# Sink attention followed by mixture-of-experts attention on one core: two-bank PSUM buffers evacuated as wholes, values in pairs of rows, and a new order of steps

## The chip, the core and the metric

The kernel runs on one core of a Trainium2 chip. The metric is device time in microseconds (us) of one execution. The kernel before took 470.62, 473.53 and 476.29 us in three runs, a median of 473.53. Its engines are PE (TensorE: matmuls, with PEld as its weight loads), DVE (VectorE), ACT (ScalarE), POOL (GpSimd) and SP (SyncE, which issues all DMAs). Matmul results land in PSUM, which here is cut into buffers; DVE and ACT can read them, POOL cannot.

## What is computed

Two attention layers, one after the other, in fp32. The first has 4 batches of 8 heads, 768 positions and a head size of 64; each position sees the 4 first positions ("sinks") and the last 128. Its output, with the heads side by side, is the x of the second.

```
scores = q @ k.T / 8;  keep = (pos_k < 4) | (0 <= pos_q - pos_k < 128)
a = softmax(where(keep, scores, -1e9));  x = a @ v          # x: 4 x 768 x 512
logits = x @ w_gate                                          # 4 experts, the best 2 are kept
w = softmax over the kept logits
for e in experts:
    q, k, v = x @ wq[e], x @ wk[e], x @ wv[e]                # 512 -> 64
    ye = softmax(causal(q @ k.T / 8)) @ v @ wo[e]
    out += w[e] * ye
```

## The kernel before

**Precision.** A product that needs fp32 is made of three matmuls of a split number: each operand is a high part (rounded) and a low part (the rest), and high x high, high x low and low x high are added up in PSUM (the tuple `THREE`). So every copy of such an operand out of PSUM is two instructions: ACT writes the high part, DVE subtracts it for the low part.

**Units of work.** `first(b, hp)` is the first attention for one batch and one pair of heads: 4 x 4 units. It loads q, k and v, turns q and k (in the first batch by PE, later by DVE), and works through six rows of 128 queries. `values(b)` multiplies x with wv and the gate weights for all six rows, then ranks the experts on DVE. `second(b, ep)` is the second attention for one pair of experts: 4 x 2 units. It first projects x to q and k, then works through six causal rows. `store(b, i)` multiplies the result by wo, two rows of 128 at a time, and sends them out.

A row of either attention passes PE four times in effect: scores (L497), transposing the probabilities (L545), attention times values (L518), with softmax between the first two: mask and minimum on DVE (L642, L709, L744), exponential on ACT (L650, L714, L748), reciprocal on DVE, scaling by POOL (L657, L721, L763). After the transposes ACT or DVE copies the result to SBUF (L395, L397). In the first attention two rows beyond the second go together (`both_rows`).

**PSUM.** There are three buffers named `s` of 1024 fp32 columns, which are two banks each, and two named `acc` of one bank, for attention times values. Everything else that PE writes goes to an `s` buffer: scores of a row (one bank for each head), transposes, projections, values and stores. One of them is taken when its first step is placed, and is free when its last user is done.

- A projection (L836, in `second`) has one `s` buffer for q and one for k. Four row blocks (512 columns) fill the first bank with 12 matmuls, the last two blocks (256 columns) half of the second with 12 more. `pair.put` then copies: ACT L442 the high part, DVE L445 the low part, once for 512 columns and once for 256. Its destination is written with a pattern of four dimensions.
- Values (L867) put one row into each bank, 12 matmuls of 260 columns; after each row its 256 value columns are copied (L395 or L397) and its 4 gate columns (L875).
- Stores (L912) put one row into each bank, 12 matmuls of 512 columns, each copied to an `o` tile (L395 or L397) and sent.

In each of these, the copies of the first bank depend on the matmuls of that bank alone.

**The order.** The whole program is recorded as steps (`plan.step`) with a priority, a cost in ns for each engine that can do it, the steps it follows and the buffers it takes or uses. `Plan.emit` then runs through them once and puts them in an order for every engine, always the step that can begin first; on PE a step's key is its priority, plus `STAY` if it changes the kind of matmul, plus `HURRY` for every 100 ns that PE would wait. Each engine then runs its instructions strictly in that order. Priorities come from a table of some thirty numbers near L931 (`LEAD_*`, `WIDE_*`, `PREP_*`, `UNIT_*`, `STORE` and so on) and from two strings, `ORD` and `LAST`, which say how the units of `first` (a digit), the second attention of the batch before (`p`) and of the last batch (`c`) take turns. The costs in these steps are the planner's alone; they set nothing but the order.

The semaphores that hold the engines back are put in by the framework below, from the order and from the tiles that the instructions touch.

## Time and profile before

| | us |
|---|---|
| runs shown | 470.62, 473.53, 476.29 (median 473.53) |
| the profiled execution | 475.6 |
| its span, first to last instruction | 473.6 |
| busy in it: PE | 415.6 (88%) |
| busy: DVE, ACT, POOL | 312.0, 289.1, 264.4 |
| mean granted clock of PE | 0.948 |

How to read it: a span is cut into groups of instructions by source line (L836 is line 836 of the kernel before). "Idle before" is time in which the engine had nothing to run just before an instruction, put down to the instruction on another engine whose end released it. The granted clock is 1.0 at full speed; at 0.5 PE runs at half its rate. The chain of work is the path of instructions and waits that ended last, followed back from the end.

### The profile page before, as it was taken

How to read it: one execution, taken by the hardware profiler on the slowest of the kernel's cores; microseconds unless marked ns; L12 is line 12 of the kernel's file. 1: busy time of each engine (PE TensorE's matmuls, PEld its weight loads, DVE VectorE, ACT ScalarE, POOL GpSimd, SP SyncE). 2: the span in 40 equal slices, each digit the busy share in tenths (PEclk: the TensorE clock that was granted, in tenths of full speed). 3: DMA queues.
4: the chain of work that ended last, by engine and by line, in shares of the span. 5: the costliest groups of instructions: out<-in, count | busy, mean ns of one | idle time of the engine just before them, and what ended most of it. 6: DMA issues, size and time to landing. Idle time of an engine off the chain costs nothing.

```text
span 473.6 us, 12733 instructions
## 1 busy us (share of the span) xinstructions
PE 415.6 (88%) x4516; PEld 337.9 (71%) x4516; DVE 312.0 (66%) x1280; ACT 289.1 (61%) x922; POOL 264.4 (56%) x406
## 2 busy tenths in 40 slices
PE   6779989989879998999879998799879978999985
PEld 5668768877657777868657777678658766787773
DVE  4887975679929985459829985459835731546752
ACT  4897975468847976149947882428925822414840
POOL 8677986857785776037875764327821620007840
PEclk9767987989989999999999999999997998999999
DMA  8997662271054124232054100031000000003012
GB/s 177 225 151 135 125 133 36 35 134 37 1 90 78 35 36 69 60 125 52 3 83 85 35 3 1 1 134 36 3 0 1 1 1 0 3 24 113 1 46 89
DMA packets 124031, 28.41 MB, mean 60 GB/s; under 512 B 120576, under 2 KB 120576, under 8 KB 123968
## 3 DMA queue, kind: packets, MB, share of 16 engines
q1 hardware_dynamic: 123968, 27.61, 27.9%
q8 instruction: 35, 0.57, 0.5%
q14 instruction: 28, 0.23, 0.2%
HBM read 21.05 MB, written 6.29 MB: 58 GB/s over the span
## 4 chain that ended last, share of the span: by engine, by line
PE 62%; DVE 20%; ACT 11%; issue 5%; POOL 2%; DVEq 0%; ACTq 0%; POOLq 0%
PE s L836 15%; PE acc L518 13%; PE s L497 10%; PE s L912 8%; PE s L867 7%; PE s L545 7%; DVE p L642 3%; ACT pt L395 3%; DVE pt L585 2%; ACT p L650 2%; DVE p L744 2%; ACT p L748 2%; DVE pt L397 1%; DVE s L737 1%; DVE qs L445 1%
## 5 line engine op out<-in xcount | busy, mean ns | idle before, releaser
L497 PE MATMUL s<-ks,qs 64*128 64x260 f32 (+4 forms) x960 | 102.6, 336 | 11.6 <-ACT pt L395 3.2
L497 PEld LDWEIGHTS s<-ks,qs 64*128 64x128 f32 x960 | 74.7, 202 | 29.2 <-DVE st L709 5.9
L657 POOL TENSOR_TENSOR p<-p,st 128x128 f32<-128x128 f32 (+5 forms) x96 | 87.5, 933 | 2.7
L395 ACT ACTIVATE pt<-s 128x512 f32<-128x512 f32 (+1 forms) x132 | 67.9, 534 | 34.2 <-PE s L545 13.5
L537 POOL TENSOR_TENSOR st<-st,gate 128x2 f32<-128x2 f32 x48 | 9.2, 195 | 118.5 <-DVE gate L899 62.7
L650 ACT ACTIVATE p<-p,st 128x128 f32<-128x128 f32 (+5 forms) x96 | 63.5, 662 | 12.8 <-DVE st L642 12.0
L545 PE MATMUL s<-ident,p 64*128 64x64 f32 x1120 | 59.7, 234 | 3.5 <-POOL p L721 0.7
L545 PEld LDWEIGHTS s<-ident,p 64*128 64x128 f32 x1120 | 47.2, 144 | 15.0 <-issue 8.1
L642 DVE CUSTOM_DVE_ANT_0 p<-s,cmask 128x512 f32<-128x512 f32 (+3 forms) x96 | 50.2, 551 | 8.7 <-PE s L497 7.3
L748 ACT ACTIVATE p<-p,st 128x132 f32<-128x132 f32 x128 | 50.4, 399 | 0.4 <-DVE st L744 0.2
L518 PE MATMUL acc<-pt,v 128*64 128x128 f32 x672 | 48.9, 284 | 0.8 <-ACT pt L395 0.6
L836 PE MATMUL s<-x,wkh 128*128 128x256 f32 (+1 forms) x128 | 36.7, 373 | 13.1 <-ACT ks L442 6.8
L518 PE MATMUL acc<-pt,vn 128*64 128x128 f32 x448 | 45.8, 305 | 0.0
L836 PE MATMUL s<-x,wqh 128*128 128x256 f32 (+1 forms) x128 | 34.9, 358 | 12.0 <-ACT qs L442 6.4
L518 PEld LDWEIGHTS acc<-pt,v 128*64 128x64 f32 x672 | 36.2, 138 | 7.6 <-ACT pt L395 1.9
L867 PE MATMUL s<-wvh,x 128*128 128x260 f32 x192 | 38.3, 291 | 1.4 <-DVE v L397 0.5
L445 DVE TENSOR_TENSOR ks<-s,ks 128x384 fp32r<-128x384 f32 (+2 forms) x24 | 13.2, 553 | 38.7 <-PE s L836 29.4
L912 PE MATMUL s<-woh,y 128*128 128x512 f32 x96 | 33.7, 407 | 4.4 <-ACT o L395 2.1
L836 PEld LDWEIGHTS s<-x,wkh 128*128 128x128 f32 x128 | 23.6, 203 | 19.5 <-ACT ks L442 8.4
L836 PEld LDWEIGHTS s<-x,wqh 128*128 128x128 f32 x128 | 21.6, 190 | 18.2 <-ACT qs L442 7.8
L867 PEld LDWEIGHTS s<-wvh,x 128*128 128x128 f32 x192 | 30.7, 188 | 3.8 <-DVE gate L875 1.5
L763 POOL TENSOR_TENSOR p<-p,st 128x512 f32<-128x512 f32 x32 | 33.3, 1039 | 0.0
(116 smaller groups left out, 912.6 us busy)
## 6 DMA issues: line engine op xcount, KB each, us to landing
vn<-in_v_dram SPq DMA_DIRECT2D x32, 192.0 KB, 3.0
out_dram<-o SPq DMA_DIRECT2D x24, 256.0 KB, 2.0
qn<-in_q_dram SPq DMA_DIRECT2D x52, 96.0 KB, 2.3
kn<-in_k_dram SPq DMA_DIRECT2D x52, 96.0 KB, 2.3
qn<-in_q_dram SPq DMA_DIRECT2D x6, 192.0 KB, 4.1
kn<-in_k_dram SPq DMA_DIRECT2D x6, 192.0 KB, 4.4
o<-in_moe_wo_dram SPq DMA_DIRECT2D x2, 256.0 KB, 4.3
v<-in_moe_wv_dram SPq DMA_DIRECT2D x4, 128.0 KB, 2.8
```

What stands on the lines that cost most here:

```text
L395: nc.scalar.activation(dst(), src(), AF.Copy)
L497: nc.tensor.matmul(o, self.qs.t[hs, a, qs], self.ks.t[hs, b, ks], start=n == 0, stop=n == 2)
L518: nc.tensor.matmul(o[e * 64:e * 64 + 64], lhs, rhs, start=e not in self.begun, stop=last and i == self.hi - 1)
L545: nc.tensor.transpose(t.t[:, g, n, :], x[gs], ident[gs, gs])
L642: nc.vector.tensor_tensor_reduce(out=p.t[:, cs], in0=s2.t[:, e, :(c1 - c0) * 128], in1=mask[:, cs], scale=times, scalar=st.t[:, 3, es] if ...
L650: nc.scalar.activation(x, x, AF.Exp, bias=st.t[:, 0, es], scale=-1.0, accum_out=st.t[:, 1, es])
L657: nc.gpsimd.tensor_mul(x, x, st.t[:, 2, e:e + 1].to_broadcast([128, n * 128]))
L748: nc.scalar.activation(p.t[:, n, :], p.t[:, n, :], AF.Exp, bias=st.t[:, 0, n:n + 1], scale=-1.0, accum_out=st.t[:, 1, n:n + 1])
L763: nc.gpsimd.tensor_mul(p.t[:, :, :128], p.t[:, :, :128], f()[:, :, None].to_broadcast([128, 4, 128]))
L836: nc.tensor.matmul(t.t[:, at:at + n], w[a][:, c, es], X[b, c].t[:, x, cs], start=c == 0 and m == 0, stop=c == NCH - 1 and m == 2)
L867: nc.tensor.matmul(ps()[:, :VW], X[b, c].t[:, a, qs], W["wv"][w][:, c, :], start=c == 0 and n == 0, stop=c == NCH - 1 and n == 2)
L912: nc.tensor.matmul(t.t[:, r, :], Y[b, c].t[:, a, qs], W["wo"][w][:, c, :], start=c == 0 and n == 0, stop=c == EP - 1 and n == 2)
```

## The change

- In `second`, the projections of both parts of a buffer come first; the four copies follow, each waiting for the last matmul of **both** parts. The copies' source and destination are flat (`flat=True`), two dimensions in place of four.
- In `values`, nothing is copied after the first row of a buffer. After the second, one instruction copies 2 x 256 value columns and one copies 2 x 4 gate columns. The second row's matmuls follow the first's.
- In `store`, both rows' matmuls come first, then both copies.
- The planner's table of numbers is another one: costs of transposes (for instance 109 to 62 ns a block), of the switch between kinds of matmul, of ranking, the priorities, and the two strings of turns. The work of the instructions themselves does not change by it, only their order.

The core of the diff; of the table two lines stand for the rest:

```diff
-        def put(self, which, lo, hi, src, t, prio, after):
+        def put(self, which, lo, hi, src, t, prio, after, flat=False):
...
             def to(a):
+                if flat:
+                    return self.tile(which).t[:, a, lo * 128:hi * 128]
                 return self.part(which, a, lo, hi).rearrange("p j (g c) -> p j g c", c=64)
...
-            t = buf("s", 1024)
+            t, puts = buf("s", 1024), []
...
-                new, used = pair.fresh(which)
+                new, used = ([], [pair.tile(which)]) if lo else ([pair.tile(which)], [])
...
-                pair.put(which, lo, hi, lambda t=t, n=n, at=at: t.t[:, at:at + n].rearrange("p (j g c) -> p j g c", g=2, c=64), t, prep_prio, [last])
+                puts.append((lo, hi, lambda t=t, n=n, at=at: t.t[:, at:at + n], t, prep_prio, last))
+            for lo, hi, src, t, prep_prio, _ in puts:
+                pair.put(which, lo, hi, src, t, prep_prio, [x[-1] for x in puts], flat=True)
...
-                made, last = i % 2 == 0, None
+                made, before, last = i % 2 == 0, None if i % 2 == 0 else last, None
...
-                V2_READY[b].append(evacuate(prio, lambda i=i: v2.t[:, i, :], lambda ps=ps: ps()[:, :E * D], E * D, [last],
-                                            [t, v2]))
-                logits.append(plan.step(prio, {DVE: 190}, lambda i=i, ps=ps: nc.vector.tensor_copy(
-                    gate.t[:, 0, i, :], ps()[:, E * D:VW]), [last], [gate] if i == 0 else [], [t] + ([gate] if i else [])))
+                if made:
+                    continue
+                V2_READY[b] += [evacuate(prio, lambda i=i: v2.t[:, i - 1:i + 1, :], lambda t=t: t.t[:, :, :E * D], 2 * E * D, [before, last],
+                                         [t, v2])] * 2
+                logits.append(plan.step(prio, {DVE: 190}, lambda i=i, t=t: nc.vector.tensor_copy(
+                    gate.t[:, 0, i - 1:i + 1, :], t.t[:, :, E * D:VW]), [before, last], [gate] if i == 1 else [], [t] + ([gate] if i > 1 else [])))
...
-                                 [last] + [x for cc in range(EP) for x in over(Y_READY[b, cc], i + r, i + r + 1)] + W_READY["wo"],
+                                 [last, before] + [x for cc in range(EP) for x in over(Y_READY[b, cc], i + r, i + r + 1)] + W_READY["wo"],
                                  [t] if made else [], [Y[b, c]] + ([] if made else [t]), mode="FULL")
+            before = last
+            done.append((r, o, qs))
+        for r, o, qs in done:
             moved = evacuate(prio + 0.1 * r, lambda o=o: o.t, lambda r=r: t.t[:, r, :], Dm, [last], [t], [o])
...
-    WIDE_S, WIDE_E, WIDE_N = 16.27, -11.64, 15.51
+    WIDE_S, WIDE_E, WIDE_N = 14.65, 1.07, 15.16
...
-    LAST = "1 0 p0 2 3 p1 c0 c1"
+    LAST = "0 p0 1 2 3 p1 c0 c1"
```

What it does to the order is shown at three places. In these rows a name ends in its buffer's number (`s_120`, `s_121`, `s_122` are the three two-bank buffers); the semaphores in brackets are those that the row waits for, by the engine that raises them; lines of the changed kernel stand some three to seven further down (L836 is L839 there, L442 is L445, L497 is L500).

PE, the second bank (256 columns) of the q projection of the last unit, and the first matmul of the k projection behind it; before:

```order
L836 MATMUL s_122<-x_76,wqh 128x256 x2
L836 MATMUL s_122<-x_76,wql 128x256
L836 MATMUL s_122<-x_77,wqh 128x256 [waits Activation_49]
L836 MATMUL s_122<-x_77,wqh 128x256
L836 MATMUL s_122<-x_77,wql 128x256
L836 MATMUL s_122<-x_79,wqh 128x256 x2
L836 MATMUL s_122<-x_79,wql 128x256
L836 MATMUL s_122<-x_78,wqh 128x256 [waits DVE_49]
L836 MATMUL s_122<-x_78,wqh 128x256
L836 MATMUL s_122<-x_78,wql 128x256
L836 MATMUL s_120<-x_76,wkh 128x512 x2
```

and now:

```order
L839 MATMUL s_121<-x_76,wqh 128x256 x2
L839 MATMUL s_121<-x_76,wql 128x256
L839 MATMUL s_121<-x_77,wqh 128x256 x2
L839 MATMUL s_121<-x_77,wql 128x256
L839 MATMUL s_121<-x_79,wqh 128x256 x2
L839 MATMUL s_121<-x_79,wql 128x256
L839 MATMUL s_121<-x_78,wqh 128x256 x2
L839 MATMUL s_121<-x_78,wql 128x256
L839 MATMUL s_122<-x_76,wkh 128x512 [waits DVE_49]
```

The two waits inside the buffer are gone. One wait stands at the start of the next buffer, for its last user.

ACT, the copies of the same unit's q and k and what follows them; before:

```order
L442 ACTIVATE qs_72<-s_122 128x512 [waits PE_49]
L442 ACTIVATE qs_72<-s_122 128x256 [waits DVE_49,PE_49]
L442 ACTIVATE ks_75<-s_120 128x512 [waits PE_49]
L442 ACTIVATE ks_75<-s_120 128x256 [waits DVE_49,PE_49]
L650 ACTIVATE p_88,st_119<-p_88,st_119 128x384 [waits DVE_49]
```

and now:

```order
L445 ACTIVATE qs_72<-s_121 128x512 [waits PE_49]
L445 ACTIVATE qs_72<-s_121 128x256
L445 ACTIVATE ks_75<-s_122 128x512 [waits PE_49]
L445 ACTIVATE ks_75<-s_122 128x256
L396 ACTIVATE pt_99<-s_120 128x512 [waits DVE_49,PE_49,Activation_49]
```

ACT's second copy of a buffer no longer waits, neither for PE nor for DVE.

PE, from the last matmuls of a k projection to the first scores that need it, in the unit of the second batch's second expert pair (its k is `ks_73`); before:

```order
L836 MATMUL s_122<-x_76,wkh 128x256 [waits DVE_49]
L836 MATMUL s_122<-x_76,wkh 128x256
L836 MATMUL s_122<-x_76,wkl 128x256
L518 MATMUL acc_124<-pt_100,v_0_82 64x128 x4
L497 MATMUL s_120<-ks_73,qs_70 128x128 x6
```

and now:

```order
L839 MATMUL s_122<-x_77,wkl 128x256
L548 MATMUL s_120<-ident,psk_102 128x64 [waits DVE_49,Pool_49]
L548 MATMUL s_120<-ident,psk_102 128x64
L548 MATMUL s_120<-ident,p_92 128x64 [waits Pool_49]
L548 MATMUL s_120<-ident,p_92 128x64 x7
L521 MATMUL acc_123<-pt_95,vn_68 64x128 [waits DMAHW7_49]
L521 MATMUL acc_123<-pt_95,vn_68 64x128 [waits DMAHW0_49]
L548 MATMUL s_121<-ident,p_85 128x64 [waits DVE_49,Pool_49]
L548 MATMUL s_121<-ident,p_85 128x64 x3
L521 MATMUL acc_123<-pt_96,vn_68 64x128 x4
L525 MATMUL acc_123<-sk_105,vs_107 128x128 x2
L500 MATMUL s_121<-ks_73,qs_70 128x128 [waits Activation_49]
```

Before, four matmuls stood between the projection and its scores. Now the transposes of two rows, attention times values and the sinks' part of it (L525) stand between them.

More of the change, by code (lines that the diff above doesn't have):

```diff
@@ L26 @@
                 (POOL, POOL): 102, (SP, SP): 0})
-SWITCH = {(a, b): {"full": 150, "FULL": 196, "cols": 149, "rows": 196}[b]
-          for a in ("full", "FULL", "cols", "rows") for b in ("full", "FULL", "cols", "rows") if a.lower() != b.lower()}
-HURRY = 25.28
-STAY = 25.06
+SWITCH = {(a, b): {"ROWS": 150, "FULL": 198, "cols": 149, "rows": 196}[b]
+          for a in ("ROWS", "FULL", "cols", "rows") for b in ("ROWS", "FULL", "cols", "rows") if a.lower() != b.lower()}
+SWITCH["ROWS", "rows"] = 52
+HURRY = 28.13
+STAY = 30.7
 class Buf:
@@ L82, in __init__, with step @@
         self.fifo = {}
-    def step(self, prio, cost, fn, after=(), new=(), use=(), fifo=None, moves=0, mode="full", behind=()):
+    def step(self, prio, cost, fn, after=(), new=(), use=(), fifo=None, moves=0, mode="FULL", behind=()):
         s = Step(prio, cost, fn, after, new, use, moves, mode, behind)
@@ L124, in emit @@
         left = len(self.steps)
-        moved, mode = 0.0, "full"
+        moved, mode = 0.0, "FULL"
         while left:
@@ L469, in turn_by_pe @@
             new, used = self.fresh(which)
-            tt = plan.step(prio, {PE: 109 * (hi - lo)}, tr, after, [t] + new, [nat] + used,
+            tt = plan.step(prio, {PE: 62 * (hi - lo)}, tr, after, [t] + new, [nat] + used,
                            fifo=("prep", ("qs", "ks")[which]) if new else "prep", mode="ROWS")
@@ L582, in tr @@
                 turned(t, n, p.t[:, n, :128])
-        tt = plan.step(prio, {PE: 545}, tr, normed + kept, [t, whole, part, sk], [p, psk], mode="ROWS")
+        tt = plan.step(prio, {PE: 307}, tr, normed + kept, [t, whole, part, sk], [p, psk], mode="ROWS")
         halves = lambda x: x.t.rearrange("p n (g c) -> p n g c", g=2)
@@ L597, in transposed_band @@
         new, used = acc.bufs()
-        acc.steps.append(plan.step(prio + AV_LAG - 0.01, {PE: 224}, of_sinks, [moved_sk, low_sk, made_vs], new, [sk, vs] + used,
+        acc.steps.append(plan.step(prio + AV_LAG - 0.01, {PE: 170}, of_sinks, [moved_sk, low_sk, made_vs], new, [sk, vs] + used,
                                    fifo="av", mode="rows"))
@@ L899, in weigh @@
                 nc.vector.tensor_mul(wt, wt, col()[:, :, None].to_broadcast([128, m, E]))
-            s = plan.step(prio, {DVE: 1970}, rank, logits, [lots] if lo == 0 else [], [gate] + ([lots] if lo else []))
+            s = plan.step(prio, {DVE: 2800}, rank, logits, [lots] if lo == 0 else [], [gate] + ([lots] if lo else []))
             s = plan.step(prio, {ACT: 120}, lambda lo=lo, hi=hi: nc.scalar.activation(gate.t[:, 2, lo:hi], gate.t[:, 0, lo:hi], AF.Exp),
                           [s], (), [gate])
-            WT_READY[b] += [[plan.step(prio, {DVE: 1400}, weigh, [s], (), [gate])]] * m
+            WT_READY[b] += [[plan.step(prio, {DVE: 2000}, weigh, [s], (), [gate])]] * m
     def store(b, i, prio):
-        t = buf("s", 2, 512)
+        t, done, before = buf("s", 2, 512), [], None
         for r in range(2):
@@ L927 @@
     plan.step(-99.0, {PE: 2800.0}, busy, (), [idle])
[L931 to L935 removed]
+    LEAD_S, LEAD_E, LEAD_N = 18.93, -4.6, 5.94
+    WIDE_S, WIDE_E, WIDE_N = 14.65, 1.07, 15.16
+    ROW = 3.46
+    UNIT_1, UNIT_2, AV_LAG = 12.92, 24.91, 48.69
+    SINK_VALUES = 2.5
     SINKS = sink_values() if banded else None
```

12 lines of the change are left out of this document (4 added, 8 removed).

## The prediction, made before the changed kernel was run

> **What bounds the kernel now.** I read the table of stages first: which engine is full, and at which clock TensorE (PE) ran. Each row gives length, then busy microseconds (and instruction count) of PE, PEld, DVE, ACT and POOL, then granted clock, DMA share and GB/s.
>
> ```profile
> 0.00:62.24 62.24, 50.90 (x600) 41.86 (x602) 48.40 (x229) 49.41 (x178) 48.74 (x96) 0.84 0.83 159
> 62.24:410.00 347.76, 310.06 (x3346) 252.56 (x3342) 231.08 (x940) 214.26 (x684) 191.82 (x275) 0.96 0.22 44
> 410.00:473.60 63.60, 54.65 (x582) 43.48 (x578) 32.51 (x113) 25.45 (x63) 23.86 (x36) 0.99 0.14 51
> sum 473.60, PE 415.61 PEld 337.90 DVE 311.99 ACT 289.12 POOL 264.42; mean PE 138.54 PEld 112.63 DVE 104.00 ACT 96.38 POOL 88.14
> ```
>
> In the first 62 us four engines share the load (PE 82%, the others 78%); after that PE is 89% busy and DVE, the next, 66%. PE's queue sets the end there, and its idle time, 473.6 - 415.6 = 58.0 us, is the stock that a new order can draw on. The groups by line say where it lies: last in each row is the idle time before the group, with its releasers.
>
> ```profile
> L497 PE MATMUL s<-ks,qs 64*128 64x260 f32 (+4 forms) x960 | 102.6, 336 | 11.6 <-ACT pt L395 3.2 <-DVE st L709 2.8 <-DVE st L642 1.7
> L545 PE MATMUL s<-ident,p 64*128 64x64 f32 x1120 | 59.7, 234 | 3.5 <-POOL p L721 0.7 <-ACT pt L395 0.7 <-DVE ks L445 0.5
> ...
> L867 PE MATMUL s<-wvh,x 128*128 128x260 f32 x192 | 38.3, 291 | 1.4 <-DVE v L397 0.5 <-ACT v L395 0.5 <-DVE gate L875 0.2
> L836 PE MATMUL s<-x,wkh 128*128 128x256 f32 (+1 forms) x128 | 36.7, 373 | 13.1 <-ACT ks L442 6.8 <-DVE ks L445 6.3
> L836 PE MATMUL s<-x,wqh 128*128 128x256 f32 (+1 forms) x128 | 34.9, 358 | 12.0 <-ACT qs L442 6.4 <-DVE qs L445 5.5
> L912 PE MATMUL s<-woh,y 128*128 128x512 f32 x96 | 33.7, 407 | 4.4 <-ACT o L395 2.1 <-DVE o L397 1.6 <-DVE st L533 0.8
> ```
>
> More than half of the idle time stands before L836 (projections), L912 (stores) and L867 (values), and the releasers are the copies out of the very buffers that these lines write. One projection in order of time shows how:
>
> ```profile
> 346.04 0.40 PE L836 MATMUL s<-x,wqh 128*128 128x256 f32 x2
> ...
> 346.59 0.60 ACT L442 ACTIVATE qs<-s 128x512 fp32r<-128x512 f32 x1 [1.35 <-PE s L836]
> ...
> 347.24 0.50 PE L836 MATMUL s<-x,wqh 128*128 128x256 f32 x2 [0.69 <-ACT qs L442]
> ...
> 347.69 0.39 PE L836 MATMUL s<-x,wqh 128*128 128x256 f32 x2
> ...
> 348.30 0.69 DVE L445 TENSOR_TENSOR qs<-s,qs 128x512 fp32r<-128x512 f32 x1 [2.58 <-PE s L836]
> ...
> 349.05 0.50 PE L836 MATMUL s<-x,wqh 128*128 128x256 f32 x2 [0.85 <-DVE qs L445]
> ```
>
> At 346.04 PE is already writing the second bank (256 columns). ACT reads the first (512 columns), yet starts only when PE's group has ended; PE goes on only when ACT has ended, and the same happens with DVE at 348.30. So the two banks of one buffer are handed to and fro as one thing: 0.69 and 0.85 us of standing PE a time. The table of waits counts these, and what they do to the readers' queues (total, times, longest):
>
> ```profile
> ACT ks L442 <- PE s L836: 34.1, 15, 4.3
> ...
> PE s L836 <- ACT ks L442: 6.8, 8, 2.0
> PE s L836 <- ACT qs L442: 6.4, 7, 1.8
> PE s L836 <- DVE ks L445: 6.3, 7, 1.2
> ...
> PE s L836 <- DVE qs L445: 5.5, 7, 0.9
> ```
>
> Twenty-nine waits in 16 projection buffers. ACT stands at the head of its queue meanwhile (34.1 us for K's copies alone), with exponentials behind it, and DVE likewise, with masks.
>
> **The change part by part.**
>
> *Waits inside a buffer.* In the order of the change no projection's second bank waits for a copy of its first, and no second row of a pair (values, stores) does either: the matmuls of a buffer run through, and the copies follow. Removed: 6.8 + 6.4 + 6.3 + 5.5 = 25.0 us at L836, 2.1 + 1.6 = 3.7 at L912, 0.5 + 0.5 + 0.2 = 1.2 at L867: **29.9 us**.
>
> *Restarts.* After a wait the first two matmuls of 256 columns take 0.50 us (347.24), in the stream 0.39 (347.69): 0.11 us. With 29 waits and some 5 at the stores (3.7 us at 0.7 each), 34 x 0.11 = **3.7 us**.
>
> *The clock.* Stages cut where the granted clock changes:
>
> ```profile
> 72.47:79.30 6.83, 6.75 (x51) 5.97 (x53) 3.41 (x21) 3.58 (x13) 2.99 (x5) 0.50 0.17 28
> ...
> 96.37:99.78 3.41, 3.41 (x36) 3.19 (x36) 1.90 (x6) 1.53 (x4) 0.68 (x2) 0.50 0.98 156
> 130.50:133.91 3.41, 1.58 (x12) 1.18 (x11) 1.22 (x4) 1.81 (x5) 3.41 (x6) 1.00 0.22 36
> 133.91:137.33 3.42, 3.42 (x11) 2.66 (x10) 0.42 (x1) 2.03 (x5) 3.42 (x6) 0.50 0.49 79
> 352.36:355.77 3.41, 1.87 (x13) 1.39 (x11) 0.69 (x1) 0.60 (x1) 0.00 (x0) 1.00 0.00 0
> 355.77:362.60 6.83, 6.83 (x66) 5.45 (x66) 2.37 (x12) 3.37 (x12) 0.95 (x3) 0.50 0.01 2
> 393.32:396.73 3.41, 1.87 (x13) 1.49 (x12) 0.69 (x1) 0.71 (x2) 0.00 (x0) 1.00 0.00 0
> 396.73:400.14 3.41, 3.41 (x10) 2.66 (x9) 0.42 (x1) 0.27 (x1) 0.00 (x0) 0.50 0.00 0
> 294.33:297.75 3.42, 1.72 (x12) 1.64 (x13) 2.21 (x8) 1.06 (x4) 1.76 (x2) 1.00 0.00 0
> ```
>
> The stage before 133.91 holds two projection waits and only 1.58 us of PE work in 3.41; right behind it the clock is half. The same before 355.77 and 396.73 (1.87 us each), and in the chain of work the half-clock stages of 72.47 and 96.37 begin on the heels of projection waits too. Together the five last 6.83 + 3.41 + 3.42 + 6.83 + 3.41 = 23.9 us. The price, from the chain of work, one projection's 18 matmuls at half clock and at full:
>
> ```profile
> 133.42 5.32 PE s L836 x18
> ...
> 349.05 3.73 PE s L836 x18
> ```
>
> 1.6 us for a stage of 3.4, so at most 23.9 x 0.47 = 11.2 us, if everything in these stages follows the clock; none, if the dips come anyway (the last row of stages is as thin and is followed by no dip). I take **8**, nearer the upper end, because five of five follow waits that go.
>
> The Trainium skill (TensorE: Matmul & The Clock Gate, "HAM oscillation") says that the clock falls after an idle gap of more than about 3.4 us. No idle gap here reaches 2 us, so by that rule these dips owe nothing to the waits and the 8 falls out of the sum; the rows show half clock after windows that were merely half empty, which is why the row decides.
>
> *Fewer, wider copies and flat patterns.*
>
> ```profile
> L445 DVE TENSOR_TENSOR ks<-s,ks 128x512 fp32r<-128x512 f32 x8 | 5.5, 691 | 30.7 <-PE s L836 29.4 <-ACT ks L442 1.4
> ...
> L442 ACT ACTIVATE ks<-s 128x512 fp32r<-128x512 f32 x8 | 4.8, 595 | 14.9 <-PE s L836 14.9
> ...
> L395 ACT ACTIVATE o<-s 128x512 f32<-128x512 f32 x7 | 4.2, 595 | 12.4 <-PE s L912 12.4
> ...
> L445 DVE TENSOR_TENSOR ks<-s,ks 128x256 fp32r<-128x256 f32 x8 | 3.4, 424 | 7.9 <-ACT ks L442 7.9
> ...
> L442 ACT ACTIVATE ks<-s 128x256 fp32r<-128x256 f32 x8 | 3.1, 383 | 19.3 <-PE s L836 19.3
> ```
>
> The store's copy is flat already and takes the 595 ns of the patterned one: flatness is worth nothing. Two value copies of 256 columns become one of 512: on DVE 2 x 424 against 691 ns, 0.16 us saved, twelve times (less on ACT: 2 x 383 against 595), and half of the small gate copies go too. That is some 2 us and a little more, hidden under PE (DVE after the change 312 of some 437, 71%). Uncovered it would be worth those 2 us; I take 0.
>
> *What is late next.* A buffer's copies now start only after its last matmul: 0.60 + 0.38 on ACT, then 0.69 + 0.42 on DVE, some 2.3 us with the handing over. Queued behind PE's first scores of an expert pair are all of PE's later matmuls, so this is paid whenever PE reaches those scores sooner. The order puts work of other units in between: for six of the eight pairs several rows of transposes, scores and attention-times-values; for two of them one row of transposes and one of values, which the chain prices so:
>
> ```profile
> 389.40 0.81 PE acc L518 x12
> ...
> 458.70 0.89 PE s L545 x24
> ```
>
> 0.9 + 0.8 and two changes of kind: close to 2.3, not above it. Bounds: below, the new order may also close other idle time (a third of the 11.6 us ahead of the score matmuls, L497: -4); above, all eight K copies stand bare, 8 x 2.3 = +18. I take the two thin ones as bare: 2 x 2.3, rounded to **+5**.
>
> *Moved weights, stores and units.* The issue queue is the same up to its 25th row, so the first 62 us, shared by four engines, stay; weights come a few rows earlier among loads that are not waited for. Stores and the units of the last batch change place only; the last two stores end the program as before, the row copies now on two engines. Together 0, within a microsecond.
>
> Sum, against this execution: 473.6 - 29.9 - 3.7 - 8 + 5 = 437.0 of span, and with the 2.0 us around it (475.6 - 473.6) 439.0, that is 36.6 less. The median shown, 473.53, lies 2.1 below this execution: 473.5 - 36.6 = **437 us**.
>
> **The rivals.**
>
> *The wait only moves.* PE runs through its buffer and then stands before the scores for the copies. For it: three buffers of this kind in all, and 2.3 us of copies. Against it: the cover that the order shows. All eight bare and no gain in clock: 473.5 - 29.9 - 3.7 + 18 = 458.
>
> *The clock keeps its dips.* For it: 294.33, a half-empty stage without a dip, so thinness alone does not decide. Against it: five of five. 437 + 8 = 445.
>
> *Nothing gained.* The 29 waits might be for inputs (x, weights) that only end with the copies. Against it: releasers are copies of the same buffer, and PE restarts 0.05 us after ACT's end at 347.19. It would leave 473.
> The Trainium skill (PSUM — Partial Sum Buffer, "PSUM bank collisions raise a hardware error") says that engines on different banks do not disturb each other, which speaks against the need for this change; the trace shows that this program waited all the same.
>
> *Slower: transposes come too close behind their scores.* The order is made with new numbers; if it puts a row's transposes (L545) ahead of POOL's scaling of that row, PE's queue stops there.
>
> ```profile
> L763 POOL TENSOR_TENSOR p<-p,st 128x512 f32<-128x512 f32 x32 | 33.3, 1039 | 0.0
> ```
>
> There are 128 such groups (16 x 4 and 8 x 8); now they wait 3.5 us together, 0.03 each. From 36.6 / 128 = 0.29 us each the gain is eaten; at 0.4, two fifths of one scaling, it is 473.5 - 36.6 + 51 = 488. Against it: in the new order the distances between scores and transposes, counted in matmuls, are much as they were.
>
> **How the numbers follow.** Forecast (425 to 450) 0.60; clock keeps its dips (445) 0.12; the wait moves (458) 0.16; nothing gained 0.05; slower 0.07. Low end: the full clock term and the other idle time too, 473.5 - 29.9 - 3.7 - 11.2 - 4 = 425; high end the moved wait, 458. Runs of this kernel differ by 1.2% (470.62 to 476.29), so 1% is about what can be told from no change. Faster 0.60 + 0.12 + 0.16 = 0.88, same 0.05, slower 0.07.
>
> **What would show it.** Idle time before L836's matmuls near 0 to 3 us instead of 25, and ACT's second copy of a buffer right behind its first; PE idle 58 down to some 30 us; clock above 0.948, without dips behind projections. Wrong would be: PE idle before score matmuls grown from 11.6 by more than 10 us, released by L445 copies (moved wait), or idle before L545 grown beyond 30, released by POOL (slower).

## The result and the profile after

The changed kernel takes 435.75 us (median of four runs, 434.65 to 437.76). The kernel before, run beside it, takes 474.91 (470.62 to 477.14). The ratio is 0.919, with a 95% interval of 0.9112 to 0.9268: the change takes 39.2 us away. 437 was predicted, within 425 to 458. Of the 47 executions of the kernel before that ran beside the experiments, the three slowest (478.57 us and more) count as slow runs and are left out of what follows.

The profiled execution of the changed kernel took 436.12 us, with a span of 434.3. First the page's line of busy times, then the idle time of PE by line and the stages, in the columns that the prediction explains. In the changed kernel L836 is L839, L867 is L872, L912 is L919, L497 is L500, L545 is L548, L442 and L445 are L445 and L448, L395 and L397 are L396 and L398.

```profile
PE 399.3 (92%) x4516; PEld 335.6 (77%) x4516; DVE 306.1 (70%) x1256; ACT 288.5 (66%) x922; POOL 263.1 (61%) x406
```

```profile
L500 PE MATMUL s<-ks,qs 64*128 64x260 f32 (+4 forms) x960 | 104.0, 341 | 12.1 <-ACT pt L396 3.5 <-DVE st L747 3.0 <-DVE sk L594 2.3
L548 PE MATMUL s<-ident,p 64*128 64x64 f32 x1120 | 59.0, 232 | 4.8 <-DVE st L645 1.5 <-DVE pt L398 1.4 <-DVE ks L448 0.4
...
L872 PE MATMUL s<-wvh,x 128*128 128x260 f32 x192 | 36.1, 286 | 0.6 <-DVE sk L594 0.4 <-DVE st L645 0.2
L839 PE MATMUL s<-x,wqh 128*128 128x256 f32 (+1 forms) x128 | 32.5, 343 | 0.0
L839 PE MATMUL s<-x,wkh 128*128 128x256 f32 (+1 forms) x128 | 31.5, 335 | 0.0
L919 PE MATMUL s<-woh,y 128*128 128x512 f32 x96 | 31.2, 397 | 0.0
...
L548 PE MATMUL s<-ident,psk 64*128 64x64 f32 x64 | 8.6, 262 | 4.7 <-ACT pt L396 3.1 <-DVE st L747 0.9 <-POOL wql L341 0.6
```

```profile
0.00:62.24 62.24, 51.25 (x580) 43.02 (x580) 47.82 (x224) 48.37 (x170) 46.91 (x94) 0.81 0.77 150
62.24:372.60 310.36, 294.22 (x3351) 248.13 (x3349) 226.16 (x920) 212.27 (x684) 192.46 (x277) 0.97 0.25 51
372.60:434.30 61.70, 53.80 (x594) 44.48 (x590) 32.08 (x114) 27.82 (x71) 23.73 (x36) 0.99 0.14 53
```

The span went from 473.6 to 434.3, 39.3 less. Of that, 23.0 is idle time of PE (58.0 to 35.0) and 16.3 is busy time (415.6 to 399.3), with the same 4516 matmuls. Ahead of projections and stores PE now never stands: 13.1, 12.0 and 4.4 us have become 0.0, 0.0 and 0.0. The middle stage is 95% busy where it was 89%. The first 62 us hold no more work than before: 580 matmuls instead of 600, at a clock of 0.81 instead of 0.84.

The chain of work shows the projections as unbroken blocks (us from the start, length), and the table of waits (total, times, longest) what became of ACT's standing ahead of K's copies (34.1 us before):

```profile
162.68 8.53 PE s L839 x48
...
227.17 8.54 PE s L839 x48
...
348.86 16.70 PE s L839 x96
```

```profile
ACT ks L445 <- PE s L839: 17.6, 7, 3.3
DVE ks L448 <- ACT ks L445: 16.4, 7, 3.1
```

Forty-eight matmuls, q and k of one unit, take 8.53 us, and the four buffers of two units follow each other in 16.70. ACT still waits for PE there, but PE no longer waits for ACT inside a projection. ACT's share of the chain of work is 12%, before it was 11%.

### The profile page after: what moved, and what is told of

It is laid out like the page before. It is cut to its first block, busy times and chain, and to the rows that moved or that the text cites. A ratio compares the mean times of both kernels' runs of the same rounds, so it can differ in the third digit from the quotient of the medians.

```text
span 434.3 us, 12737 instructions
## 1 busy us (share of the span) xinstructions
PE 399.3 (92%) x4516; PEld 335.6 (77%) x4516; DVE 306.1 (70%) x1256; ACT 288.5 (66%) x922; POOL 263.1 (61%) x406
## 3 DMA queue, kind: packets, MB, share of 16 engines
q1 hardware_dynamic: 123968, 27.61, 30.3%
## 4 chain that ended last, share of the span: by engine, by line
PE 58%; DVE 15%; ACT 12%; POOL 8%; issue 5%; DMA 1%; DVEq 0%; POOLq 0%; ACTq 0%
PE s L839 15%; PE s L500 12%; PE acc L521 10%; PE s L919 7%; PE s L548 7%; PE s L872 6%; ACT pt L396 4%; DVE pt L588 3%; ACT p L751 2%; POOL p L660 2%; DVE p L645 2%; DVE pt L398 2%; DVE p L747 2%; ACT p L653 1%; DMA qn<-in_q_dram 1%
## 5 line engine op out<-in xcount | busy, mean ns | idle before, releaser
L500 PE MATMUL s<-ks,qs 64*128 64x260 f32 (+4 forms) x960 | 104.0, 341 | 12.1 <-ACT pt L396 3.5
L500 PEld LDWEIGHTS s<-ks,qs 64*128 64x128 f32 x960 | 76.7, 205 | 29.7 <-ACT pt L396 7.9
L396 ACT ACTIVATE pt<-s 128x512 f32<-128x512 f32 (+1 forms) x129 | 65.5, 529 | 17.7 <-DVE pt L588 6.8
L548 PE MATMUL s<-ident,p 64*128 64x64 f32 x1120 | 59.0, 232 | 4.8 <-DVE st L645 1.5
L548 PEld LDWEIGHTS s<-ident,p 64*128 64x128 f32 x1120 | 47.5, 142 | 14.1 <-issue 5.6
L724 POOL TENSOR_TENSOR p<-p,st 128x256 f32<-128x256 f32 (+1 forms) x32 | 26.4, 835 | 21.9 <-PE s L500 5.3
L872 PE MATMUL s<-wvh,x 128*128 128x260 f32 x192 | 36.1, 286 | 0.6 <-DVE sk L594 0.4
L588 DVE TENSOR_TENSOR pt<-s,own 128x512 f32<-128x512 f32 x32 | 22.0, 688 | 15.8 <-PE s L548 8.8
L839 PE MATMUL s<-x,wqh 128*128 128x256 f32 (+1 forms) x128 | 32.5, 343 | 0.0
L521 PEld LDWEIGHTS acc<-pt,vn 128*64 128x64 f32 x448 | 26.7, 147 | 6.9 <-issue 2.9
L717 ACT ACTIVATE p<-p,st 128x128 f32<-128x128 f32 (+1 forms) x64 | 28.5, 448 | 5.1 <-DVE st L712 4.8
L747 DVE CUSTOM_DVE_ANT_0 p<-s,pair_mask 128x132 f32<-128x132 f32 x128 | 31.0, 288 | 0.7
L839 PE MATMUL s<-x,wkh 128*128 128x256 f32 (+1 forms) x128 | 31.5, 335 | 0.0
```

The source lines that it names most:

```text
L396: nc.scalar.activation(dst(), src(), AF.Copy)
L500: nc.tensor.matmul(o, self.qs.t[hs, a, qs], self.ks.t[hs, b, ks], start=n == 0, stop=n == 2)
L521: nc.tensor.matmul(o[e * 64:e * 64 + 64], lhs, rhs, start=e not in self.begun, stop=last and i == self.hi - 1)
L548: nc.tensor.transpose(t.t[:, g, n, :], x[gs], ident[gs, gs])
L588: tri = plan.step(prio, {DVE: 65 + 1.04 * 512}, lambda: nc.vector.tensor_mul(part.t.rearrange("p n (g c) -> p g n c", g=2), t.t[:, :, :4, ...
L747: nc.vector.tensor_tensor_reduce(out=p.t[:, n, :], in0=s2.t[:, e, :SW], in1=pair_mask, scale=-scale, scalar=BIG, op0=OP.add, op1=OP.min, a ...
```

## The experiments

Two things come in one change: the copies of a buffer wait for both banks, and a new table of numbers makes the order anew. The theory of the prediction is that the waits inside the buffers carry the gain. Its rival is that the order carries it (other idle time closed, other neighbours). The first two kernels are the missing corners (old order without the waits, new order with them), the next two the halves of the change.

### Old order, the waits inside the buffers taken away

Here every engine keeps the sequence of the kernel before. Only the recording order between engines is turned, so that the copies of the first bank come behind the last matmul of the second, wherever that can be had without a circle (`relink` sorts the recorded steps once more under these conditions):

```diff
+            (_, copies), (later, others) = parts
+            plan.moves.append(([later[-1]] * 2, copies, [(x, y) for x in later for y in copies] + [(others[0], copies[1])]))
...
-        for _, _, s in order:
+        for _, _, s in self.relink(order):
```

> The kernel before, with every engine's instructions in exactly the order of before; only the recording between the engines is moved, so that in all 16 projection buffers the copies are recorded behind the last matmul. 25 of the 29 waits inside a buffer go, those of values and stores mostly stay. Theory A (the waits inside a buffer carry the gain, the new order little): some 25 waits of 0.77 us and 0.3 us of stopping and starting each, and a few us of clock: 475 - 27 - 5 = 443 (437 to 449), PE idle before L836's successors under 3 us. Rival B (the new order carries the gain, the waits would only move): 465 to 475, with the idle time now before the scores.

Measured: 444.85 us (443.75 to 446.83), ratio 0.9394 (0.9324 to 0.9465). Thirty of the 39 us are there with no instruction moved on any engine. The waits at values and stores, which were expected to stay mostly, went too (0.5 and 0.0 us are left). PE by line in this kernel, whose scores are L569 and projections L909:

```profile
L569 PE MATMUL s<-ks,qs 64*128 64x260 f32 (+4 forms) x960 | 106.8, 342 | 16.6 <-DVE ks L517 5.5 <-ACT pt L467 3.0 <-DVE st L781 2.3
...
L909 PE MATMUL s<-x,wqh 128*128 128x256 f32 (+1 forms) x128 | 32.9, 347 | 0.2
L909 PE MATMUL s<-x,wkh 128*128 128x256 f32 (+1 forms) x128 | 31.4, 335 | 0.0
```

The 25.0 us ahead of the projections are 0.2. In their place 5.5 us stand before the scores, released by DVE's copies of K: the wait has moved, as the prediction's rival had it, but only a fifth of it.

### New order, the waits put back

The changed kernel, linked the other way round: the copies ACT and DVE make of the first bank stand ahead of the second bank's second and fourth step again.

```diff
+            high, low = pair.ready[which][-2][2][:2]
+            plan.moves.append(([high, low], [parts[1][1], parts[1][3]], [(x, y) for x in parts[1] for y in (high, low)] + [(pair.ready[which][-1][2][0], low)]))
```

> The changed kernel, with every engine's instructions in exactly its order; only the recording is moved back, so that in 13 of the 16 projection buffers the copy of the first bank is recorded in the midst of the second bank's matmuls, as before the change (28 waits inside buffers instead of 3). Theory A: 25 waits of 0.77 us and 0.3 us each, and some clock: 436 + 27 + 4 = 467 (460 to 473). Rival B: within 5 us of the changed kernel, 436 to 441.

Measured: 474.07 us (471.24 to 475.01), ratio 0.9996 (0.9957 to 1.0035). Everything is lost again, a microsecond more than the expected range. PE's projections in this kernel (L912) stand as they did before the change:

```profile
L912 PE MATMUL s<-x,wkh 128*128 128x256 f32 (+1 forms) x128 | 37.5, 381 | 12.4 <-ACT ks L517 7.3 <-DVE ks L520 5.1
...
L912 PE MATMUL s<-x,wqh 128*128 128x256 f32 (+1 forms) x128 | 35.4, 362 | 14.3 <-ACT qs L517 8.4 <-DVE qs L520 6.0
```

Twenty-six waits (7 + 6 + 7 + 6 in the table of waits), 26.7 us, no wait put back at values or stores: 38.3 us more than the changed kernel. Some 4 of these are the clock's, by the price worked out further down: time at half clock, a mean over the runs, is 55.6 us, in the changed kernel 43.0. So the new order is worth nothing while the waits are in it.

### Late copies under the old numbers, and the new numbers alone

The first of these two takes the change's `put`, `second`, `values` and `store` into the kernel before and leaves its table of numbers; the second does the reverse. In both the planner makes the order itself.

```diff
+            for lo, hi, src, t, prep_prio, _ in puts:
+                pair.put(which, lo, hi, src, t, prep_prio, [x[-1] for x in puts], flat=True)
...
     WIDE_S, WIDE_E, WIDE_N = 16.27, -11.64, 15.51
```

> The change without its new table of numbers: copies after both banks, values in pairs, flat patterns, but the planner keeps the priorities, costs and strings of turns of before. Theory A: most of the gain, 437 to 447. Rival B: 460 to 475.

```diff
                 pair.put(which, lo, hi, lambda t=t, n=n, at=at: t.t[:, at:at + n].rearrange("p (j g c) -> p j g c", g=2, c=64), t, prep_prio, [last])
...
-    WIDE_S, WIDE_E, WIDE_N = 16.27, -11.64, 15.51
+    WIDE_S, WIDE_E, WIDE_N = 14.65, 1.07, 15.16
```

> The new table of numbers alone, with the copies of a bank where they were, after that bank's own matmuls. 27 waits inside projection buffers come out of the planner. Theory A: 465 to 480, like before. Rival B: 436 to 450.

Measured: late copies under old numbers 437.24 us (436.63 to 441.39), ratio 0.9248 (0.9171 to 0.9325); new numbers alone 474.94 (472.49 to 477.68), ratio 1.0024 (0.9974 to 1.0074). PE in the two kernels (projections L838, then L837):

```profile
L499 PE MATMUL s<-ks,qs 64*128 64x260 f32 (+4 forms) x960 | 101.9, 335 | 15.4 <-DVE st L711 3.4 <-ACT pt L395 3.0 <-DVE ks L447 2.8
...
L838 PE MATMUL s<-x,wkh 128*128 128x256 f32 (+1 forms) x128 | 31.5, 335 | 0.0
```

```profile
L837 PE MATMUL s<-x,wkh 128*128 128x256 f32 (+1 forms) x128 | 35.0, 358 | 12.7 <-DVE ks L446 7.2 <-ACT ks L443 5.5
...
L837 PE MATMUL s<-x,wqh 128*128 128x256 f32 (+1 forms) x128 | 34.2, 353 | 8.2 <-ACT qs L443 4.8 <-DVE qs L446 3.4
```

The table of numbers is worth nothing by itself, and at most a microsecond or two on top of the late copies (437.24 against 435.75, with intervals that overlap). The new numbers set a little more than the order: alone, they also hand six copies from ACT to DVE (916 and 1286 instructions, before 922 and 1280). What is worth something is that the planner knows of the dependency: with the waits gone and the order untouched the time was 444.85, with the same numbers and an order planned around late copies 437.24, 7.6 less. That kernel also copies values in pairs, which the other does not, so the 7.6 are not the planning's alone. The stop for K's copies ahead of the scores falls from 5.5 to 2.8 us by that. The corners side by side:

| us | waits inside the buffers | none |
|---|---|---|
| old order | 474.91 | 444.85 |
| new order | 474.07 | 435.75 |

### Patterned copies

The change with its copies patterned as before, everything else alike:

```diff
-                puts.append((lo, hi, lambda t=t, n=n, at=at: t.t[:, at:at + n], t, prep_prio, last))
+                puts.append((lo, hi, lambda t=t, n=n, at=at: t.t[:, at:at + n].rearrange("p (j g c) -> p j g c", g=2, c=64), t, prep_prio, last))
...
-                pair.put(which, lo, hi, src, t, prep_prio, [x[-1] for x in puts], flat=True)
+                pair.put(which, lo, hi, src, t, prep_prio, [x[-1] for x in puts])
```

> The changed kernel with the projections' copies in the four-dimensional pattern of before; every engine's order is the same as in the changed kernel. The prediction's step (flat patterns are worth nothing): within 0.5% of the changed kernel, 434 to 438. Rival (flat patterns shorten the copies or free DVE from a wait): 439 to 446, with the 512-column copies some 10% longer than 595 and 691 ns.

Measured: 435.83 us (434.39 to 436.35), ratio 0.9176 (0.9129 to 0.9224), 0.1 from the changed kernel. The flat copies of the changed kernel and the patterned ones take the same time, first flat, then patterned:

```profile
L445 ACT ACTIVATE ks<-s 128x512 fp32r<-128x512 f32 x8 | 4.8, 597 | 17.6 <-PE s L839 17.6
```

```profile
L445 ACT ACTIVATE ks<-s 128x512 fp32r<-128x512 f32 x8 | 4.8, 597 | 17.7 <-PE s L839 17.7
```

### One wait back

As the second kernel, but only ACT's copy of the first bank goes back between the second bank's steps, so that each of the 16 projection buffers has one wait in place of up to two. This prices one stop.

```diff
-            plan.moves.append(([high, low], [parts[1][1], parts[1][3]], [(x, y) for x in parts[1] for y in (high, low)] + [(pair.ready[which][-1][2][0], low)]))
+            plan.moves.append(([high], [parts[1][1]], [(x, y) for x in parts[1] for y in (high, low)] + [(pair.ready[which][-1][2][0], low)]))
```

> The changed kernel in its own order, with only ACT's copy of the first bank recorded in the midst of the second bank's matmuls, in all 16 projection buffers: 16 waits inside buffers in place of the 25 put back in the run before, DVE's are left out. Theory A1 (each wait costs its own length of 0.69 us and some 0.3 us of draining and restarting PE, and half clock comes with thin stages): 436 + 16 x 1.0 + 4 = 456 (450 to 461), the same price of about 1.3 to 1.5 us a wait. Rival A2 (the price is the length of the wait and 0.11 us alone): 436 + 16 x 0.8 = 449 (447 to 450).

Measured: 454.45 us (452.99 to 455.92), ratio 0.9573 (0.951 to 0.9635). PE's busy time in this kernel and in the one with patterned copies, and the waits of this one:

```profile
PE 400.5 (89%) x4516; PEld 334.1 (74%) x4516; DVE 303.9 (67%) x1256; ACT 290.1 (64%) x922; POOL 263.5 (58%) x406
```

```profile
PE 397.2 (92%) x4516; PEld 334.1 (77%) x4516; DVE 305.4 (71%) x1256; ACT 288.6 (67%) x922; POOL 263.7 (61%) x406
```

```profile
PE s L912 <- ACT qs L517: 9.1, 8, 2.7
PE s L912 <- ACT ks L517: 8.2, 8, 3.4
```

Sixteen waits cost 18.6 us against the kernel with patterned copies, the nearest in clock (39.2 and 39.7 us of half clock, mean of their runs): 1.16 each. The idle time counted at the waits is 17.3 us, single waits being up to 3.4 long. PE is also busy 3.3 us longer (400.5 against 397.2), though it issues the same matmuls at the same clock: 0.21 us a stop. Of the 3.3, 3.1 lie at the projections (107.1 us in the patterned kernel, 110.2 here), where the stops are. The 4 us that were expected for more half clock did not come.

### Projections alone

The changed kernel with `values` and `store` as before, new numbers included:

```diff
-                if made:
-                    continue
-                V2_READY[b] += [evacuate(prio, lambda i=i: v2.t[:, i - 1:i + 1, :], lambda t=t: t.t[:, :, :E * D], 2 * E * D, [before, last],
-                                         [t, v2])] * 2
+                V2_READY[b].append(evacuate(prio, lambda i=i: v2.t[:, i, :], lambda ps=ps: ps()[:, :E * D], E * D, [last],
+                                            [t, v2]))
...
-            done.append((r, o, qs))
-        for r, o, qs in done:
```

> The changed kernel with values and stores as before (each row's copy recorded behind that row), projections and the table of numbers as in the change. Their waits in the profile of before: 3.7 us at the stores and 1.2 at the values, with 0.3 us of draining and restarting each 7 us. Theory A: 441 to 445. Rival (they hide under PE's other work): 434 to 438.

Measured: 440.08 us (439.56 to 442.55), ratio 0.9283 (0.9211 to 0.9355), a microsecond below the expected range: pairs of rows at values and stores are worth 4.3 us, the projections the other 35. PE's two groups in it:

```profile
L872 PE MATMUL s<-wvh,x 128*128 128x260 f32 x192 | 38.0, 290 | 0.9 <-DVE sk L594 0.3 <-DVE st L645 0.2 <-DVE gate L880 0.2
...
L917 PE MATMUL s<-woh,y 128*128 128x512 f32 x96 | 32.8, 404 | 3.7 <-ACT o L396 2.1 <-DVE o L398 1.6
```

3.7 us of waits at the stores have come back, and the matmuls of these two groups take 1.9 and 1.6 us longer.

### The clock: filling thin stages

The prediction had half clock follow stages in which PE is only half busy. The five kernels of this part test that, and whether anything is left there to gain: they add matmuls by a tile of zeros ahead of groups of transposes, into columns that nobody reads. This is work added to the computation; the output does not change. The first adds two ahead of each of the first batch's 32 groups of transposes:

```diff
+    def fill(t):
+        for g in range(2):
+            for _ in range(1):
+                nc.tensor.matmul(t.t[:, g, 5:7, :], nought, nought, start=True, stop=True)
...
             def tr():
+                fill(t)
                 for j in range(hi - lo):
...
         def tr():
+            if early:
+                fill(t)
...
-            band_rows(prio_of, pair, value, b * HP + hp, finish, groups)
+            band_rows(prio_of, pair, value, b * HP + hp, finish, groups, b == 0)
```

> The changed kernel with added work: two matmuls of zeros (128 x 128) ahead of each group of transposes in the first attention of the first batch, 32 groups, all in the first 62 us. They stand in front of the wait that PE has there anyway, and write columns that nobody reads. Theory C (PE's half clock follows stages in which PE has little to do, and costs time): the 24 us of half clock in the first 62 us shrink by half or more, and the time falls by 2 to 6 us, 430 to 434. Rival C1 (half clock has another cause): half clock as it was, and time up by up to the 64 x 0.21 = 13 us of added matmuls, 438 to 449. Rival C2 (half clock goes, but PE does not set the pace there): clock better, time within 2 us of the changed kernel.

The next three place them otherwise. Each cut is against the first of these kernels. Only ahead of the first batch's transposes of probabilities (16 groups, 32 matmuls):

```diff
             def tr():
-                fill(t)
                 for j in range(hi - lo):
```

> As the run with zero matmuls before, but ahead of the 16 groups of transposed probabilities in the first batch only (32 added matmuls, some 7 us of PE). There 64 of them took all half clock out of the first 62 us and the kernel was 4 us slower: 13.6 us added, some 10 won. If the dips end with half the filling, 7 added against up to 10 won: 431 to 435. If the dips stay where nothing is filled (half clock in the first 62 us above 12 us): 436 to 441.

Only ahead of those of q and k (16 groups, 32 matmuls):

```diff
-            band_rows(prio_of, pair, value, b * HP + hp, finish, groups, b == 0)
+            band_rows(prio_of, pair, value, b * HP + hp, finish, groups, False)
```

> The same 32 added matmuls, but ahead of the 16 groups of transposed q and k of the first batch. Same two readings: dips gone, 431 to 435; dips stay, 436 to 441.

Ahead of those of probabilities in two batches (64 matmuls), with the line at the transposes of q and k left out as in the cut for 16 groups of probabilities:

```diff
-            band_rows(prio_of, pair, value, b * HP + hp, finish, groups, b == 0)
+            band_rows(prio_of, pair, value, b * HP + hp, finish, groups, b <= 1)
```

> Zero matmuls ahead of the 32 groups of transposed probabilities of the first two batches (64 added, 13.6 us), so that they reach the dips behind 62 us too (41 us of half clock in all in the changed kernel, worth some 18 us if PE sets the pace in all of it). If the clock sets the time: half clock under 12 us, 430 to 436. If the added matmuls cost as much as the clock gives: 438 to 445.

The last halves the best of these, one matmul ahead of each q and k group:

```diff
-        for g in range(2):
+        for g in range(1):
```

> The run with zero matmuls ahead of the 16 groups of transposed q and k, with one matmul a group in place of two (16 added, 3.4 us of PE). If one is enough to keep the clock up in the first 62 us: 430 to 434, a ratio to the kernel before of 0.906 to 0.914, faster than the changed kernel (0.919) and than two a group (0.916). If dips come back (half clock in the first 62 us above 10 us): 434 to 439.

Half clock here is what the granted clock of a run means: twice what lacks to 1.0, times its span, as a mean over the runs.

| filled | us | ratio (95%) | half clock, us | first projection on the chain of work, us |
|---|---|---|---|---|
| nothing (the change) | 435.75 (434.65 to 437.76) | 0.919 (0.9112 to 0.9268) | 43.0 | 68.11 |
| all groups of the first batch | 439.84 (439.13 to 439.96) | 0.9262 (0.9203 to 0.9321) | 14.0 | 71.73 |
| its probabilities | 443.83 (440.94 to 445.41) | 0.9345 (0.9284 to 0.9406) | 40.6 | 77.46 |
| its q and k | 433.58 (433.29 to 435.59) | 0.9163 (0.9112 to 0.9214) | 13.8 | 66.22 |
| probabilities of two batches | 444.60 (444.13 to 445.71) | 0.9385 (0.9345 to 0.9425) | 28.1 | 76.62 |
| q and k, one for two | 436.57 (432.89 to 437.1) | 0.9197 (0.9144 to 0.9251) | 29.0 | 69.16 |

Stages of the changed kernel, of the kernel with q and k filled, and of the one with half of that:

```profile
13.06:16.47 3.41, 1.71 (x26) 1.10 (x26) 3.34 (x17) 3.28 (x13) 1.80 (x4) 1.00 0.83 150
16.47:23.30 6.83, 6.83 (x60) 5.71 (x62) 4.65 (x25) 4.85 (x21) 4.96 (x9) 0.50 1.10 234
23.30:26.71 3.41, 1.70 (x34) 1.19 (x32) 3.24 (x15) 3.00 (x12) 0.93 (x2) 1.00 1.04 192
26.71:33.54 6.83, 5.84 (x58) 5.17 (x56) 5.52 (x26) 5.75 (x21) 6.27 (x8) 0.50 0.49 81
```

```profile
0.00:62.24 62.24, 53.20 (x644) 43.49 (x644) 48.48 (x225) 48.83 (x172) 47.79 (x95) 1.00 0.78 151
...
30.59:34.00 3.41, 2.26 (x36) 1.80 (x32) 3.31 (x22) 3.41 (x15) 3.33 (x6) 1.00 0.37 60
34.00:37.41 3.41, 3.41 (x37) 2.71 (x36) 2.39 (x11) 2.28 (x11) 2.65 (x5) 1.00 1.04 205
```

```profile
24.35:27.77 3.42, 2.39 (x32) 1.73 (x32) 3.11 (x14) 3.42 (x10) 2.60 (x4) 1.00 1.04 176
27.77:44.83 17.06, 16.12 (x130) 13.62 (x132) 12.20 (x55) 12.04 (x46) 11.47 (x17) 0.50 0.66 113
```

In the changed kernel a stage with 1.7 us of work in 3.4 is followed by half clock, every time in these rows. Its whole trace bears this out: cut into stages of 3.41 us that fit the dips, from 4 us on, the seven that lead from full to half clock hold 1.59 to 1.94 us of PE work, and the 104 that keep full clock hold 2.36 or more. With q and k filled, the first 62 us run at 1.00 throughout, so filling thin stages does take dips away. Yet 29 us less half clock bring only 2 us: the filler itself takes 11.7 us of PE (0.37 a matmul, where 0.21 was expected), and in those 62 us the other engines are nearly as full as PE, so the first projection begins at 66.22 instead of 68.11. No other filling gains anything, and three of them cost 4 to 9 us. Two of the readings set down beforehand missed: with all groups filled the half clock went as one of them had it, but the time rose by 4 us as another had it; with only the probabilities filled the time, 443.83, lies above both ranges. The interval of the best (0.9112 to 0.9214) overlaps that of the change, so none of these is shown to beat it. Where the limit lies stays open: a stage with 2.26 us of work kept the clock, one with 2.39 us was followed by 17 us at half, and in the kernel before one with 1.72 us kept it (294.33), so the busy time of a stage is not quite what decides.

## Why the prediction held, point by point

**Waits inside a buffer: 29.9 predicted, 30.3 measured.** 25.1 us ahead of L836 are 0.0, 4.4 ahead of L912 are 0.0, 1.4 ahead of L867 are 0.6. The old order without them and the new order with them settle that these waits are the cause: 30 us gained without moving anything on an engine, 38 lost by putting them back (some 4 of these by the clock). They were not inputs that came late (the "nothing gained" rival): nothing about the inputs differs between those kernels.

**Restarts: 3.7 predicted, some 7 by the price of a stop that the runs gave.** This term of the sum was too small. I read only the first two matmuls behind a wait, 0.11 us. The last matmul ahead of a stop adds to it, as in these rows of the kernel before:

```profile
352.49 0.28 PE L836 MATMUL s<-x,wkl 128*128 128x256 f32 x1
353.45 0.50 PE L836 MATMUL s<-x,wkh 128*128 128x256 f32 x2 [0.69 <-ACT ks L442]
353.79 0.28 PE L836 MATMUL s<-x,wkl 128*128 128x256 f32 x1
353.91 0.40 PE L836 MATMUL s<-x,wkh 128*128 128x256 f32 x2
```

In the stream the next matmul begins 0.12 us behind the one of 353.79 and overlaps the rest of its 0.28; the one of 352.49, ahead of a stop, overlaps with nothing. (The ends of matmuls in a profile are modelled, so these sizes are rough.) Sixteen stops put back cost 3.3 us of busy time, 0.21 each, so 34 of them cost 7.1, an estimate.

**The clock: 8 predicted, 1 to 2 measured.** This is the term that was wrong. The granted clock is listed with each run. Over 44 executions of the kernel before, half clock has a mean of 46.8 us (33.7 to 60.0) and the span follows it at 0.32 us per us, with a correlation of 0.94. The four runs of the changed kernel have 43.0 us. So the change took 3.8 us of half clock away, worth 1.2 us by that slope; the two profiles differ by 6.8 (47.8 to 41.0 until PE's end), worth 2.2. Both are estimates. The step that failed is "if everything in these stages follows the clock; none, if the dips come anyway (the last row of stages is as thin and is followed by no dip). I take **8**, nearer the upper end, because five of five follow waits that go." The price was not at fault: at 0.32 the 23.9 us would be worth 7.6. The amount was. The three dips of 133.91, 355.77 and 396.73 (13.7 us) went and nothing took their place. But the two of 72.47 and 96.37 (10.2 us) were followed by two in nearly the same places, now behind waits ahead of scores and transposes (13.7 us), and the first 62 us have 3.4 us more half clock (23.9 against 20.5):

```profile
74.49:77.91 3.42, 1.59 (x20) 1.44 (x22) 2.57 (x10) 1.79 (x7) 3.42 (x6) 1.00 0.26 41
77.91:81.32 3.41, 3.41 (x32) 2.85 (x30) 2.50 (x16) 2.32 (x9) 1.95 (x4) 0.50 0.03 7
94.97:98.39 3.42, 1.80 (x31) 1.49 (x30) 3.32 (x5) 0.00 (x0) 3.42 (x6) 1.00 0.77 127
98.39:108.63 10.24, 8.92 (x76) 7.45 (x76) 8.59 (x36) 6.64 (x22) 1.18 (x5) 0.50 0.41 75
```

That projection waits do bring dips is shown by the kernel with the waits put back, in the order of the change. Behind projection waits its profile has four dips that the changed kernel lacks (132.49, 333.88, 381.67 and 402.15, 17.1 us together), for instance:

```profile
330.47:333.88 3.41, 1.87 (x12) 1.40 (x11) 1.02 (x3) 0.83 (x3) 3.17 (x6) 1.00 0.00 0
333.88:337.29 3.41, 3.41 (x10) 2.83 (x11) 0.42 (x1) 0.38 (x1) 1.95 (x4) 0.50 0.00 0
```

The rival "the clock keeps its dips" was thus nearly right about the clock, and its time of 445 was still too long, because other terms had been put too low. The reading behind my 8, half clock after half-empty stages, held: the stages above have 1.59 and 1.80 us of work, and no gap in them is longer than 2.93 us. The Trainium skill (TensorE: Matmul & The Clock Gate, "HAM oscillation") has the clock fall after an idle gap of more than about 3.4 us; these rows fall without such a gap, and filling the stages kept the clock up, so here the clock falls without what the rule asks for, and the measurement decides.

**What is late next: +5 predicted, +7.3 measured, at another place.** PE's idle time outside the removed waits went from 27.1 to 34.4. I had put it before the scores, behind K's copies; that group went only from 11.6 to 12.1. The largest piece is a single stop ahead of the transposes of the sinks' probabilities (0.8 us before, 4.7 now), in order of time:

```profile
96.74 1.72 DVE L897 TENSOR_SCALAR gate<-gate 128x24 f32<-128x24 f32 x1
...
98.37 0.17 DVE L898 TENSOR_TENSOR gate<-gate 128x24 f32<-128x24 f32 x1
...
98.58 0.22 ACT L908 ACTIVATE gate<-gate 128x24 f32<-128x24 f32 x1 [5.26 <-DVE gate L898]
...
99.71 0.37 PE L548 MATMUL s<-ident,psk 64*128 64x64 f32 x2 [2.93 <-ACT pt L396]
```

ACT stands for 5.26 us at the exponential of the expert ranking, until DVE has ranked; behind it in ACT's queue lies the copy that frees a buffer for PE's transposes. Before, ACT stood at this place too, and PE behind it, for the copy of K's first bank:

```profile
95.10 0.22 ACT L901 ACTIVATE gate<-gate 128x24 f32<-128x24 f32 x1 [2.25 <-DVE gate L891]
...
95.86 0.51 PE L836 MATMUL s<-x,wkh 128*128 128x256 f32 x2 [1.99 <-ACT ks L442]
```

So the longest of the 29 waits was the ranking's doing; it is counted among those taken away, and stands now, 2.93 us long, before the transposes. Two fifths of the 7.3 us are this one stop; most of the rest is a microsecond here and there ahead of other transposes. The order alone does not fix its size: in the kernel with patterned copies, whose order is the same, PE stood there for 0.94 us, and for 1.93 before scores 4 us later, with 35.1 us of idle time in all against 35.0. That a stop at the ranking also opens the half clock of 98.39 fits the rows but was not tried by itself.

**Flat patterns: 0 predicted, 0 measured** (435.83 against 435.75, 597 ns either way). **Wider copies** of values: 0 predicted; DVE's busy time fell by 5.9 us, to 70% of the span; the wider copy was not tried apart from the pairing. That values and stores together are worth 4.3 us is their waits and stops: 3.7 us of idle time at the stores.

**Moved weights, stores, units: 0 predicted, 0 measured** for the new numbers alone (ratio 1.0024). But an order is worth something once the copies are late: planning with that dependency known, and values copied in pairs, brought 7.6 us over the old order without waits. Nearly all of it is busy time of PE (407.1 us with the old order, 399.6 and 399.3 with the two planned ones) and hardly any is idle time (36.4, 35.3 and 35.0). The scores' matmuls alone take 106.8, 101.9 and 104.0 us. Some of that will be stops, for the old order has thirteen before the scores for K's copies; what else it is I did not take apart.

**The rest: in no term, 7.0 measured.** In the balance of the two profiles 16.3 us of busy time less 7.1 for restarts and 2.2 for the clock leave 7.0. It is not shown to be the order's. By line, 14.1 of the 16.3 us lie where the waits were: at the projections (116.2 to 106.9, summed over their groups), values (65.4 to 63.2) and stores (52.7 to 50.1), while the scores take 1.4 more (104.0 against 102.6). And putting the waits back without moving an instruction raises the busy time by 13.5 us, of which the same two prices explain only 26 x 0.21 = 5.5 and 13.6 x 0.32 = 4.4. So a stop, or a dip that falls on a projection, probably costs more than these prices; which of the two stays open.

So the balance is 30.3 + 7.1 + 2.2 + 7.0 - 7.3 = 39.3 us of span, where the prediction had 29.9 + 3.7 + 8 - 5 = 36.6. The main term was right. That the sum is 2.7 us off, and not 8.5, is luck: a clock term 5.8 too large stood in for restarts that were 3.4 too small and a rest of 7.0 that was in no term.

## What to carry to other kernels

When a framework tracks a buffer of several banks as one thing, copying one bank out while the next is being written is no overlap: each hand-over costs the copy, the signals and 0.2 us of a matmul stream that stops and starts again, 1.16 us each here. Write the whole buffer, then copy it, and tell the planner of the dependency that is really enforced: that, with values copied in pairs, was worth up to 7.6 us more, where retuned numbers without it were worth nothing. Before a gain from a higher clock is counted, ask what will fill the thin stages behind which the clock fell: taking one cause of thin stages away (23.9 us of dips) left room for others, and only 3.8 to 6.8 us of half clock went.

## What the runs showed of the hardware

- The time of one program follows its half clock at 0.32 us per us (44 executions, 33.7 to 60.0 us of half clock), though a projection with 3.42 us of half clock in it takes 1.59 us longer (5.32 against 3.73), 0.47 per us. That much of a dip falls where PE is not what is waited for would explain it, and was not tried.
- Half clock comes in steps of 3.41 us. It can stay for 17 us while PE is 95% busy (27.77 to 44.83 above). In the profiles of the kernels before and after, each of the 15 returns to full clock follows a stage with at least 3.16 us of PE work, but six stages as busy were followed by more half clock. So a busy PE does not end it at once.
- Two added matmuls ahead of each q and k group, from 5.5 us on, kept the clock full for the first 62 us; one for two kept it only until 27.77. Ahead of the probabilities alone they begin at 15.8 us, behind a first dip at 8.5, and the dips stayed (30.7 us in those 62). Their mean length is 362 ns there and 308 ahead of q and k (each is two records in the trace), and the time grew by 8 us.
